# A spectral mixer and an MLP in one kernel: one row's sums moved to ScalarE, half a table loaded instead of computed, five fewer zero matmuls, and new instruction orders

## The chip, the cores and the metric

The kernel runs on one core of one Trainium2 chip. The metric is the device time of the whole program in microseconds (us). The kernel before took 348.37 us, the median of three runs (348.06 to 348.37). The profile is one execution of 348.26 us, of which it shows a span of 346.5 us. All times of the trace count from the start of that span.

## The reference: what is computed

The input x has 2048 positions of 512 features, in bf16. Two kinds of layer follow each other, twice:

```python
x = x + _A_ref(_layernorm(x, axis=-1), A_w_r, A_w_i)   # rfft2, times W, irfft2
x = x + _B_ref(_layernorm(x, axis=-1), B_w1, B_w2, B_w3, B_w4)
x = x + _A_ref(_layernorm(x, axis=-1), A_w_r, A_w_i)
x = x + _B_ref(_layernorm(x, axis=-1), B_w1, B_w2, B_w3, B_w4)
```

`_A_ref` takes a two-dimensional real Fourier transform of the normalised x, multiplies it by the complex weight W and transforms back. `_B_ref` normalises, multiplies by w1, applies GELU, shifts the four quarters of the features by -1, +1, -2 and +2 positions, multiplies by w2, adds x, normalises again and runs an MLP of width 1792 (w3, GELU, w4) with a second addition.

## The kernel before, in words

**Layout.** The 2048 positions lie as 128 partitions p by 16 rows q (position 16p+q). A "row" in this text is one q: a tile of 128 partitions by 512 features. The state x stays in SBUF for the whole run (`x_state`).

**The front.** The forward transform begins with a DFT over p: for each row TensorE multiplies the row by a 128x256 table T, which has first been scaled by the row's reciprocal standard deviation, so that the layernorm is folded into the table. `first_front` (L433) does this for the input. Its work is spelled as letters in the string ORDER_0, in program order, and every engine runs its own instructions in that order. `s5` takes the sums of row 5: either with BATCH_NORM_STATS on DVE (L273), or, for the rows in ON_ACT, with two ScalarE passes (a Copy at L349 and a Square at L285, each with an accumulated sum). `i5` aggregates the DVE form (L301). `f1` finishes the ScalarE form for the rows of group 1 with three small GpSimd instructions per row (L355 to L357). `S1` and `J1` are the square root on ScalarE (L361) and the reciprocal on DVE (L364) for group 1. GROUPS holds rows 0-3, 4-7, 8-11, 12-13 and 14-15. `Q5V` or `Q5A` writes the scaled table of row 5 on DVE (L379) or ScalarE (L381). `O2` is the front matmuls of the third row pair (L392, L394), followed for the first five pairs by FILL[k] matmuls on zeros (L257). `G2A` or `G2V` evicts that pair from PSUM into V on ScalarE or DVE (L150, L152). O7 and O8 are the single rows 14 and 15. The eviction of row 15 is split into G8A and G8V.

**Loads.** T comes over the ScalarE queue. The x rows and the W planes come over the SyncE queue. The other tables come over the GpSimd queue through `load_rest` (L180), which is called after the whole of ORDER_0: FA, two halves of TL, half of TR, and `double(0)`, which copies the first quarter of W into the other partitions. After them a one-element copy, the `gate` (L191), waits for the last scaled table. Behind the gate stand `turn_TL` for blocks 0-7, `double(1)`, `turn_TL` for blocks 8-15, `double(2)`, `double(3)` and the rest of TR. `turn_TL` (L230) makes the second plane of TL from the first: it swaps the two columns of every pair and negates one, in two GpSimd instructions (L233, L234).

**A layer.** `layer` (L490) runs twice. Its orders are ORDER_A and ORDER_B, in the same style, with the PSUM bank written after a dot. `d` is the DFT over features (L511), `t` its eviction, `q` the step over the row index against TL (L535: plane 0 and plane 1 of TL, one matmul each), `x` its eviction, `p` the product with W on DVE (L554), `b` the way back against TR (L565), `m` its eviction into hT, `D` and `Y` the inverse over features (L583) and its eviction, `P` the inverse over p (L595), `a` the addition to x with sums (L603), `s` the squares (L285), `r`, `e`, `i` and `n` the second layernorm, `T` a transposing DMA (L623), and `v`, `h`, `u`, `f`, `w`, `g`, `W`, `A` the matmuls, GELUs and additions of the two MLPs (L635 to L712). Units 0, 1, 14 and 15 hold one block of 64 frequencies, and units 2 to 12 hold two. Unit 10 covers blocks 10 and 11 and is thus the first user of the second half of TL in both orders. A suffix V or A names the engine of an eviction. `X4` is four matmuls on zeros (L257), and `N0` negates a part of TR on DVE (L770). `L` permutes a part of W for the second layer. The end of ORDER_A already makes the front of the second layer: `B` and `j` are stats, `S`, `J`, `Q` the scaled tables, `O` and `G` the front matmuls and their evictions. The first pairs use four plain matmuls (L404) and four DVE additions (`G0V` to `G4V`, L416) that need a copy of half the bank by ScalarE first (`G0A` to `G4A`).

At the very start, WAKE zero matmuls (L252, L257) keep TensorE occupied until the first scaled table is there.

Of the kernel before, what the change touches and what calls it, by code (L numbers as in the profile page):

```python
# [16 lines left out]
P = 128  # L17
# [4 lines left out]
NB = 16  # L22
# [6 lines left out]
def dft_tables():  # L29
# [14 lines left out]
    T = np.zeros((P, NH, 2, 2))  # L44
# [5 lines left out]
    T = T.reshape(P, P)  # L50
# [6 lines left out]
    FA = np.stack([cos, -sin], axis=1).reshape(2, P, 2, P, 2)[..., ::-1].transpose(1, 0, 4, 2, 3)  # L57
# [3 lines left out]
    G = G.transpose(2, 0, 1)  # L61
# [5 lines left out]
    for j in range(NH):  # L67
        for sg in range(2):
# [86 lines left out]
def load_all(K, A_x, A_w_r, A_w_i, B_w1, B_w2, B_w3, B_w4):  # L155
# [21 lines left out]
    K.TL = K.const.tile([P, 2, NB, P], BF16, name="TL")  # L177
    K.TR = K.const.tile([P, 3, NH, 64], BF16, name="TR")

    def load_rest(after):  # L180
        q = nc.gpsimd
        load_TL = lambda k: q.dma_start(K.TL[:, 0, 8 * k:8 * k + 8], dram["TL"][:, 8 * k:8 * k + 8])
        load_TR = lambda k: q.dma_start(K.TR[:, 0:2 + k, 16 * k:16 * k + 16], dram["TR"][:, 0:2 + k, 16 * k:16 * k + 16])
        double = lambda k: q.dma_start(K.W[1::2, :, 8 * k:8 * k + 8], K.W[0::2, :, 8 * k:8 * k + 8])
        table("FA", q)
        load_TL(0)
        load_TL(1)
        load_TR(0)
        double(0)
        gate = K.const.tile([1, 2], BF16, name="gate")  # L190
        q.tensor_copy(gate[:], after[0:1, 0, 0:2])  # L191
        turn_TL(K, slice(0, 8))
        double(1)
        turn_TL(K, slice(8, 16))
        double(2)
        double(3)
        load_TR(1)

    K.load_rest = load_rest
    K.load_G2 = lambda: nc.sync.dma_start(K.G[:], dram["G2"])  # L200

    def load_mlp():
# [230 lines left out]
def first_front(K):  # L433

    new_V(K)
    K.Tq = {}
    at = {q: (g, i) for g, rows in enumerate(GROUPS) for i, q in enumerate(rows)}
    L = [Stats(K, n=len(rows)) for rows in GROUPS]
    for g, rows in enumerate(GROUPS):
        if any(q in ON_ACT for q in rows):  # L440
            L[g].sums()
    ps = {}

    last_T = None
# [24 lines left out]
    def take(k, eng):
        take_V(K, FIRST[k], ps[k], eng, k == len(FIRST) - 1)  # L470

    def means(g):
        for i, q in enumerate(GROUPS[g]):
            if q in ON_ACT:
                L[g].from_means(i)

    table = {"s": stats, "i": aggr, "f": means, "S": lambda g: L[g].std(),
             "J": lambda g: L[g].invert(), "p": lambda g: L[g].rstd(), "Q": scale, "O": front, "G": take}
    for op in ORDER_0.split():
        if op[0] in "QG":  # L480
            table[op[0]](int(op[1:-1]), op[-1])
        else:
            table[op[0]](int(op[1:]))
    K.load_rest(last_T[:])
    K.load_mlp()
    spare = K.grp.tile([P, 4, 4, P], BF16, name="xT", bufs=4)
    K.nc.sync.dma_start_transpose(spare[:, 0, 0:1], K.zeros[:])
# [305 lines left out]
            table[op[0]](int(op[1:]))  # L793


WAKE = 35
FILL = {0: 3, 1: 3, 2: 2, 3: 2, 4: 2}
GROUPS = [[0, 1, 2, 3], [4, 5, 6, 7], [8, 9, 10, 11], [12, 13], [14, 15]]
ON_ACT = [1, 5]
FIRST = [[0, 1], [2, 3], [4, 5], [6, 7], [8, 9], [10, 11], [12, 13], [14], [15]]  # L800
UNITS = {b: [b, b + 1] if 2 <= b < 14 else [b] for b in (0, 1, 2, 4, 6, 8, 10, 12, 14, 15)}
ROOT = (0, 1)
# [5 lines left out]
PLAIN = 5  # L808
FLEX = "mGnotxY"
ORDER_0 = """  # L810
s0 s2 i0 s3 s1 i2 i3 f0 s4 S0 J0 i4 s5 Q1V Q0V Q3V Q2V s7 s6 i7 i6 s9 s11 O0 G0A f1 i9 S1 J1 s8 O1 G1A Q6A s10 Q7A i11
O3 i8 i10 Q5A s13 s12 Q4A O2 S2 J2 i13 Q10V G3A i12 Q9V s15 Q11A O5 S3 Q8A s14 i15 G2A O4 i14 S4 J3 Q12V G5A J4 Q15A
Q13V O6 Q14V G6A G4V O7 G7V O8 G8V G8A
"""
ORDER_A = """
X4.1 N0 d0.3 t0A d2.5 d1.7 t1A d4.0 t4A q0.2 x0A t2V q1.4 x1V p1 d10.6 d6.4 p0 t6V q2.1 t10A q4.6 x2A p2 x4A d12.3
b1.0 q6.1 p4 q10.6 t12A m1V b3.3 m3V x6A d8.4 d14.2 d15.0 x10A b5.6 t8A q8.4 p6 t14V t15A q12.0 b2.7 p10 m2V q14.2 m5A
x8A x12A q15.4 b0.6 m0A b10.7 m10A b4.1 m4A p8 b6.0 p12 m6V x14A p14 b11.7 x15A b9.1 p15 b13.6 m11A m9V m13A b7.3
b12.5 m12A b8.2 m8A b14.7 m14A m7V b15.5 m15A m15V D1.1 Y1V D0.5 D3.3 P2.7 a2 P3.2 a3 Y0A P0.1 a0 Y3A P7.4 P1.7 a1 s2
P6.2 s3 D2.0 s0 s1 a7 s7 a6 s6 D5.3 D4.6 r0 e0 Y2V P4.5 Y5A Y4A i0 n0V n1V P5.0 a4 s4 a5 s5 P11.2 D7.4 r1 P10.6 T0 Y7A  # L820
P8.3 e1 n3V n2V c1 T1 a11 a8 i1 D6.0 Y6A n5V P9.4 s11 P14.7 n4V n6V a9 n7V T2 P15.5 P12.3 a10 s8 a15 s9 a14 s10 P13.0
L0 v0.1 h0 a12 a13 v1.5 h1 T3 r2 c2 v3.4 n11V s12 c0 n10V T5 n8V n9V h3 s15 v2.3 h2 u0.5 L8 u3.0 u2.7 f0 L2 s14 f3
u1.5 f1 s13 r3 n12V n14V n15V f2 T4 v5.2 n13V h5 v4.1 u4.5 f4 E1 h4 u7.6 u6.1 f7 E3 u5.4 T7 k1 k0 f6 f5 k3 k2 E5 R0 c3
T6 v7.5 h7 u15.7 E0 v6.0 h6 E6 E4 u8.4 k7 o0V k5 o1V f15 E2 k6 o2V u10.3 o3V f10 k10 u12.7 u11.0 f8 u14.1 f14 U0 U1
u9.2 f9 k9 k8 w2.4 g2 f12 L9 E9 k4 R1 f11 k11 R2 w5.6 E11 g5 w4.2 g4 w1.0 u13.4 E8 o8V g1 o9V w3.5 g3 f13 E10 o10V
w0.1 g0 E7 o4A o7V w6.3 g6 W2.2 z0 o5V o6V A2 W3.7 A3 W1.6 A1 B1 W0.2 U3 U4 U2 E14 A0 w8.6 L13 B3 j3 g8 k14 o11V w12.1
g12 U5 w13.6 g13 w7.3 g7 w9.6 g9 k15 w10.3 g10 w18.0 w15.3 E12 g18 g15 w14.6 g14 w16.0 L11 w11.3 g11 g16 B2 W6.2 E13
W4.0 A6 w20.5 k13 L5 A4 B4 L12 W7.0 g20 w17.4 k12 R3 g17 o13A W5.1 A5 w19.5 g19 W9.2 o12V U6 j1 A7 B7 L15 j7 E15 j2 L7
o15V B6 W8.1 j6 B0 B5 j5 L3 W10.7 j0 S0 A10 B10 o14A U7 A9 j10 w25.4 g25 B9 Q2 j4 j9 A8 B8 L1 S1 Q1 Q4 w24.6 g24 W11.0
w21.2 g21 Q6 w22.6 j8 A11 L4 Q0 Q7 B11 j11 g22 L10 O0.3 w26.1 L14 g26 S2 Q11 G0A Q3 w23.6 w27.0 Q9 G0V g23 O1.2 G1A  # L830
Q10 G1V g27 W12.5 A12 O3.0 B12 W15.6 j12 Q5 G3A G3V A15 O2.2 G2A B15 Q8 j15 G2V S15 J15 Q15 W13.5 A13 B13 S12 W24.4
A24 j13 S13 J12 Q12 B24 J13 W14.5 Q13 A14 B14 O4.0 G4A O15.2 j14 S14 O5.6 G15V G15A O6.4 J14 Q14 O14.2 G4V G5A X3.7
G14V L6 G6A X4.1 G14A
"""
# [17 lines left out]


# [28 lines left out]
```

## Time and profile before

| | before |
|---|---|
| device time, median of 3 | 348.37 us |
| span of the profile | 346.5 us |
| TensorE (PE) busy | 337.5 us, 97% |
| ScalarE (ACT) busy | 192.0 us, 55% |
| VectorE (DVE) busy | 187.9 us, 54% |
| GpSimd (POOL) busy | 65.2 us, 19% |
| front: start to the first matmul of the first layer's `d` | 18.74 us |
| first layer, `d` to `b` (18.74 to 38.41) | 19.67 us |
| first layer, `D` and `P` up to the first `v` (38.41 to 53.12) | 14.71 us |
| its MLPs, and most of the second front (53.12 to 177.90) | 124.78 us |
| second layer, `d` to `b` (183.49 to 203.10) | 19.61 us |
| second layer, `D` and `P` up to the first `v` (203.10 to 218.40) | 15.30 us |

The share of TensorE is high in every stage, but a busy matmul engine is not always the one that sets the pace: the profile counts a matmul as busy for its whole latency (270 ns for 256 columns), while the next one starts much earlier. So a stage is read from the distances between starts, and from what the other engines had to do in it.

### The profile page before, as it was taken

The numbers are of one execution on the slowest core, as the hardware profiler recorded it, in microseconds if no ns is written. First come the engines' busy times: TensorE is split into PE (matmuls) and PEld (weight loads), VectorE is DVE, ScalarE is ACT, GpSimd is POOL, SyncE is SP. The second block draws the span as 40 slices with busy tenths as digits, with TensorE's granted clock in tenths as the row PEclk, the third lists the DMA queues.
The fourth block names the chain that finished last, engine by engine and source line by source line (L and its number), as shares of the span: only waits on it lengthen the run. The fifth ranks groups of instructions, "written<-read, shape, count | busy, mean of one in ns | idle before, by whom it ended". The sixth has DMA issues, their size and how long they took to land.

```text
span 346.5 us, 5563 instructions
## 1 busy us (share of the span) xinstructions
PE 337.5 (97%) x2116; PEld 190.0 (55%) x2134; DVE 187.9 (54%) x452; ACT 192.0 (55%) x342; POOL 65.2 (19%) x158
## 2 busy tenths in 40 slices
PE   8899999999999999999999999999999999999996
PEld 6778884444444444444577888444444444444453
DVE  5979798785435012877698959666614202002012
ACT  5979799666504633124357989954784531350320
POOL 2470047442200001032000003544305000000000
PEclk9999999999999999999999999999999999999999
DMA  7997965430221000210000002542103114100101
GB/s 265 290 328 246 359 132 111 80 63 7 49 45 30 0 2 0 55 38 1 0 2 0 2 2 53 95 88 50 23 2 61 30 45 104 19 30 17 45 23 53
DMA packets 45337, 24.64 MB, mean 71 GB/s; under 512 B 34944, under 2 KB 42240, under 8 KB 45312
## 3 DMA queue, kind: packets, MB, share of 16 engines
q1 hardware_dynamic: 43904, 20.00, 23.6%
q0 software_dynamic: 1168, 4.20, 3.4%
q8 instruction: 16, 0.26, 0.3%
q10 hardware_dynamic: 240, 0.10, 0.1%
q14 instruction: 9, 0.07, 0.1%
HBM read 11.67 MB, written 2.10 MB: 40 GB/s over the span
## 4 chain that ended last, share of the span: by engine, by line
PE 80%; DVE 8%; ACT 5%; DMA 4%; issue 2%; DVEq 0%; SPq 0%; ACTq 0%
PE ps L686 28%; PE ps L706 27%; PE ps L635 8%; PE ps L651 8%; PE ps L511 3%; DVE x_state L603 3%; DMA xT<-xn 2%; ACT V L152 2%; PE ps L583 2%; DVE PB L554 2%; PE ps L535 1%; DMA x_state<-in_A_x_dram 1%; DVE hT L150 1%; ACT X L152 1%; DMA T<-tab_T 1%
## 5 line engine op out<-in xcount | busy, mean ns | idle before, releaser
L693 ACT ACTIVATE gT<-ps 128x1024 bf16<-128x1024 f32 x56 | 56.3, 1022 | 93.9 <-PE ps L686 93.7
L686 PE MATMUL ps<-xT,w 128*128 128x512 bf16 x448 | 99.3, 379 | 0.1
L706 PE MATMUL ps<-w,gT 128*128 128x512 bf16 (+1 forms) x464 | 97.8, 366 | 0.6
L712 DVE TENSOR_TENSOR x_state<-ps,x_state 128x512 bf16<-128x512 f32 (+1 forms) x34 | 22.1, 657 | 108.6 <-PE ps L706 106.9
L706 PEld LDWEIGHTS <-gT 128*128 128x128 bf16 x476 | 46.5, 98 | 49.9
L686 PEld LDWEIGHTS <-w 128*128 128x128 bf16 x448 | 43.7, 98 | 52.9 <-DMA xT<-xn 0.6
L659 DVE SCALAR_TENSOR_TENSOR xn<-xn,ln_c,ps 128x512 bf16<-128x512 bf16 x32 | 23.2, 744 | 21.4 <-PE ps L651 13.1
L635 PE MATMUL ps<-xT,w 128*128 128x512 bf16 x128 | 28.8, 379 | 0.9 <-DMA xT<-xn 0.9
L651 PE MATMUL ps<-w,hT 128*128 128x512 bf16 x122 | 28.6, 379 | 0.3
L285 ACT ACTIVATE junk<-xn 128x512 bf16<-128x512 bf16 x32 | 19.7, 619 | 10.1 <-DVE xn L659 10.1
L642 ACT ACTIVATE hT<-ps 128x512 bf16<-128x512 f32 x32 | 18.1, 601 | 11.8 <-PE ps L635 11.8
L603 DVE SCALAR_TENSOR_TENSOR x_state<-ps,x_state 128x512 bf16<-128x512 f32 x32 | 20.5, 686 | 5.1 <-PE ps L595 5.1
L273 DVE BATCH_NORM_STATS2 ln_st<-x_state 128x6 f32<-128x512 bf16 (+1 forms) x31 | 20.2, 667 | 3.6 <-DMA x_state<-in_A_x_dram 3.2
L635 PEld LDWEIGHTS <-w 128*128 128x128 bf16 x128 | 12.4, 98 | 16.0 <-issue 1.6
L291 POOL TENSOR_SCALAR ln_mv<-ln_s 128x4 f32<-128x4 f32 x16 | 4.9, 304 | 85.3 <-DVE x_state L603 73.2
L651 PEld LDWEIGHTS <-hT 128*128 128x128 bf16 x128 | 12.5, 98 | 15.1
L554 DVE TENSOR_TENSOR PB<-X,W 128x2048 bf16<-128x2048 bf16 (+1 forms) x20 | 19.6, 1010 | 0.7 <-ACT X L152 0.5
L285 ACT ACTIVATE xn<-x_state 128x512 bf16<-128x512 bf16 x32 | 19.9, 624 | 0.2 <-DVE x_state L603 0.2
L293 POOL TENSOR_TENSOR ln_mv<-ln_s,ln_t 128x4 f32<-128x4 f32 x16 | 3.5, 217 | 75.4 <-ACT junk L285 70.0
L583 PE MATMUL ps<-G,hT 128*128 128x256 bf16 x128 | 15.4, 272 | 0.9 <-DVE hT L150 0.8
L565 PE MATMUL ps<-TR,PB 128*128 128x128 bf16 x256 | 16.1, 219 | 0.1
L565 PEld LDWEIGHTS <-PB 128*128 128x128 bf16 x256 | 14.8, 98 | 1.5 <-issue 1.2
(87 smaller groups left out, 390.0 us busy)
## 6 DMA issues: line engine op xcount, KB each, us to landing
w<-in_B_w_dram SPq DMA_DIRECT2D x2, 1792.0 KB, 12.1
W<-W POOLq DMA_DIRECT2D x4, 514.0 KB, 4.5
x_state<-in_A_x_dram SPq DMA_DIRECT2D x8, 256.0 KB, 4.8
out_dram<-x_state SPq DMA_DIRECT2D x15, 128.0 KB, 1.9
w<-in_B_w_dram SPq DMA_DIRECT2D x2, 512.0 KB, 6.2
W<-in_A_w_r_dram SPq DMA_DIRECT2D x7, 128.5 KB, 6.1
W<-in_A_w_i_dram SPq DMA_DIRECT2D x7, 128.5 KB, 6.5
TR<-tab_TR POOLq DMA_DIRECT2D x1, 768.0 KB, 6.8
```

The source lines that it names most:

```text
L285: K.nc.scalar.activation(out, src, ACT.Square, bias=0.0, scale=D ** -0.5, accum_out=self.s[:, i, 1:2])
L554: nc.vector.tensor_tensor(t, X.pop(u)[:, 0:2 * n].unsqueeze(1).to_broadcast([P, 2, 2 * n, 256]), K.W[:, :, 2 * u:2 * u + 2 * n, 1:257], op ...
L565: nc.tensor.matmul(oh, lhsT=pab[u][:, k, 2 * (b - u) + h, F * P:(F + 1) * P], rhs=K.TR[:, k:k + 2, 2 * b + h], start=(k == 0), stop=(k == 1))
L583: nc.tensor.matmul(o[:, i, e * 256:(e + 1) * 256], lhsT=M[:, F, e, 2 * m + i, :], rhs=K.G[:, F, e, :], start=(F == 0 and e == 0), stop=(F ...
L603: nc.vector.scalar_tensor_tensor(K.x[:, q, :], ps.pop(("P", q)), 1.0, K.x[:, q, :], op0=ALU.mult, op1=ALU.add, accum_out=ln[g].s[:, i, 0:1])
L635: nc.tensor.matmul(o[:, i], lhsT=K.w1[:, t, j * P:(j + 1) * P], rhs=xT[g][:, :, t, :], start=(t == 0), stop=(t == 3))
L651: nc.tensor.matmul(o, lhsT=K.hT[:, j, st:st + P], rhs=K.w2[:, j, :], start=(j == 0), stop=(j == 3))
L659: nc.vector.scalar_tensor_tensor(xn[:, q, :], xn[:, q, :], ln[q // 4].c[:, q % 4:q % 4 + 1], ps.pop(("u", n)), op0=ALU.mult, op1=ALU.add, ...
L686: nc.tensor.matmul(o[:, i], lhsT=K.w3[:, c, t * P:(t + 1) * P], rhs=xT3[g][:, :, c, :], start=(c == 0), stop=(c == 3))
L693: nc.scalar.activation(gT[g][:, 2 * j:2 * j + 2, :], ps.pop(("w", k)), ACT.Gelu_apprx_tanh, bias=0.0, scale=1.0)
L706: nc.tensor.matmul(o, lhsT=gT[g][:, t, i * P:(i + 1) * P], rhs=K.w4[:, t, d], start=(t == 0), stop=(t == 13))
L712: nc.vector.tensor_tensor(x, ps.pop(("W", n)), x, op=ALU.add)
```

## The change

1. **Row 9's sums.** ON_ACT gets row 9: its BATCH_NORM_STATS and aggregation leave DVE, and a Copy and a Square on ScalarE and three small GpSimd instructions (`f2`) come in.
2. **Half of the turned table.** The host makes a new table TL2, the second plane of TL for blocks 8-15. One DMA on the GpSimd queue loads it where the second `turn_TL` stood.
3. **Where the tables are loaded.** The first four table loads move into `load_tables`, which is called right after `f1`, so that `f2` stands behind them on the GpSimd queue and not ahead of them.
4. **WAKE** goes from 35 to 30 zero matmuls.
5. **New orders** for all three strings. In ORDER_0 the first table of row 1 moves from DVE to ScalarE, those of rows 4, 6, 7 and 15 from ScalarE to DVE, pair 4 is evicted by ScalarE, pair 6 by DVE and row 14 by ScalarE, as the last eviction. In ORDER_A the four zero matmuls at its start move to just ahead of the first `D`.

```diff
+    TL2 = TL.reshape(P, NB, 64, 2)[:, NB // 2:, :, ::-1] * np.array([-1.0, 1.0])
+    TL2 = TL2.reshape(P, NB // 2, P)
...
+    def load_tables():
         table("FA", q)
         load_TL(0)
         load_TL(1)
         load_TR(0)
+
+    def load_rest(after):
         double(0)
         gate = K.const.tile([1, 2], BF16, name="gate")
         q.tensor_copy(gate[:], after[0:1, 0, 0:2])
         turn_TL(K, slice(0, 8))
         double(1)
-        turn_TL(K, slice(8, 16))
+        q.dma_start(K.TL[:, 1, 8:16], dram["TL2"])
         double(2)
         double(3)
         load_TR(1)
...
+        if g == TABLES:
+            K.load_tables()
...
-WAKE = 35
+WAKE = 30
...
-ON_ACT = [1, 5]
+ON_ACT = [1, 5, 9]
+TABLES = 1
...
 ORDER_0 = """
-s0 s2 i0 s3 s1 i2 i3 f0 s4 S0 J0 i4 s5 Q1V Q0V Q3V Q2V s7 s6 i7 i6 s9 s11 O0 G0A f1 i9 S1 J1 s8 O1 G1A Q6A s10 Q7A i11
-O3 i8 i10 Q5A s13 s12 Q4A O2 S2 J2 i13 Q10V G3A i12 Q9V s15 Q11A O5 S3 Q8A s14 i15 G2A O4 i14 S4 J3 Q12V G5A J4 Q15A
-Q13V O6 Q14V G6A G4V O7 G7V O8 G8V G8A
+s0 s2 s3 i2 s1 f0 i0 i3 s4 S0 s5 f1 J0 Q3V Q0V Q2V Q1A O1 i4 s7 s9 s6 i7 i6 s11 s10 O0 S1 J1 Q7V Q4V G1A Q6V s8 G0A
+i11 f2 i10 Q5A i8 S2 s13 s12 O3 G3A J2 Q11A Q8A i12 i13 Q10V s15 S3 O2 G2A s14 i15 Q9V O5 O4 i14 J3 Q12V S4 G5A Q13V
+G4A O6 J4 Q14V O7 Q15V G6V O8 G8A G8V G7A
 """
 ORDER_A = """
-X4.1 N0 d0.3 t0A d2.5 d1.7 t1A d4.0 t4A q0.2 x0A t2V q1.4 x1V p1 d10.6 d6.4 p0 t6V q2.1 t10A q4.6 x2A p2 x4A d12.3
-b1.0 q6.1 p4 q10.6 t12A m1V b3.3 m3V x6A d8.4 d14.2 d15.0 x10A b5.6 t8A q8.4 p6 t14V t15A q12.0 b2.7 p10 m2V q14.2 m5A
...
-Q10 G1V g27 W12.5 A12 O3.0 B12 W15.6 j12 Q5 G3A G3V A15 O2.2 G2A B15 Q8 j15 G2V S15 J15 Q15 W13.5 A13 B13 S12 W24.4
-A24 j13 S13 J12 Q12 B24 J13 W14.5 Q13 A14 B14 O4.0 G4A O15.2 j14 S14 O5.6 G15V G15A O6.4 J14 Q14 O14.2 G4V G5A X3.7
-G14V L6 G6A X4.1 G14A
+d0.0 t0A d1.4 t1A d2.6 t2A q1.0 q0.2 x0A d4.4 t4A x1V p1 d10.1 N0 p0 q2.6 t10A q4.4 x4A d6.0 x2V p2 d12.3 p4 t6A q10.6
+q6.1 x6V t12A p6 b2.0 x10A p10 m2A d8.3 d14.6 t8A b3.1 m3A d15.7 t15A q8.3 x8A t14V q12.0 x12A p8 b1.5 b4.7 b7.6 m7A
...
+G3A G3V g26 G2A G2V W12.4 A12 B12 O0.2 j12 S12 L7 J12 Q12 W15.1 A15 B15 W13.5 G0A G0V j15 S15 W24.7 A13 B13 W14.5 J15
+j13 S13 A24 Q10 O4.6 G4A B24 J13 Q15 O15.1 Q13 Q11 A14 B14 j14 S14 G15V G15A O5.4 G5A J14 O6.0 Q14 O14.3 X3.5 G6A G4V
+X4.6 G14V G14A
 """
 ORDER_B = """
-d1.1 d4.3 t1V d15.7 t15V d8.0 t8V t4A q1.2 x1A p1 q4.6 x4A p4 d12.4 q15.2 t12A d10.6 x15A p15 t10A q8.0 q12.4 x12A
...
+d1.1 t1A d15.2 t15V d4.0 d8.6 t4A t8A q1.4 x1V q4.2 x4A p1 q15.0 d12.4 x15V p15 t12A d10.6 p4 q8.1 q12.3 b1.5 b5.0
...
 """
```

## The prediction

> **What bounds the kernel now.** I read the page's busy rows first, then busy time by stage, then the order-of-time view around the two places where TensorE (PE) does not set the pace. By stage (window and length, then busy time of PE, PEld, DVE, ACT, POOL, clock, DMA share, GB/s):
>
> ```profile
> 18.74:38.41 19.67, 19.15 (x258) 16.12 (x256) 17.78 (x23) 17.47 (x26) 5.30 (x7) 1.00 0.86 289
> 38.41:53.12 14.71, 14.47 (x128) 12.43 (x129) 12.39 (x35) 12.49 (x30) 3.81 (x13) 1.00 0.80 214
> 53.12:177.90 124.78, 124.31 (x601) 58.27 (x611) 71.91 (x183) 58.08 (x100) 25.08 (x55) 1.00 0.17 32
> 183.49:203.10 19.61, 19.17 (x256) 16.00 (x257) 18.02 (x22) 17.26 (x27) 0.00 (x0) 1.00 0.01 2
> 203.10:218.40 15.30, 14.51 (x128) 12.44 (x129) 11.14 (x33) 14.24 (x32) 4.51 (x15) 1.00 0.24 46
> 218.40:343.05 124.65, 124.16 (x581) 57.56 (x590) 36.46 (x93) 54.81 (x95) 19.11 (x48) 1.00 0.20 44
> ```
>
> Rows 3 and 6 are 249 us in which PE waits for nothing (0.5 us each is missing) and DVE and ACT are half idle: no order can shorten them, since the matmuls are the same. What is left is about 97 us. A 256-column matmul starts each 0.109 us (24 `D` in 2.62 us), so `D` and `P` cost 128 x 0.109 = 13.95 of the 14.71 us. `d`, `q` and `b` cost 64 x 0.109 + 64 x 0.066 + 128 x 0.056 = 18.3 of 19.67 us. All slack of the kernel is thus some 1.4 us in each `d`-`b` stage, about 1 us in each `D`-`P` stage, and the two fronts. The end of the first front, in order of time:
>
> ```profile
> 16.43 2.33 DVE L150 CAST V<-ps 128x1024 bf16<-128x1024 f32 x3
> 17.23 1.30 ACT L152 ACTIVATE V<-ps 128x1024 bf16<-128x1024 f32 x2
> 18.31 0.60 PE L257 MATMUL ps<-zeros 128*128 128x256 bf16 x4 [0.22 <-ACT V L152]
> 18.43 0.75 POOL L234 COPY TL<-TL 128x512 bf16<-128x512 bf16 x1
> 18.68 0.79 DVE L770 TENSOR_SCALAR TR<-TR 128x1024 bf16<-128x1024 bf16 x1
> 18.74 2.78 PE L511 MATMUL ps<-FA,V 128*128 128x256 bf16 x24
> ```
>
> `d` starts when the last eviction of V is done: DVE at 18.7, after working without a gap since 4.17. ACT had 0.9 us to spare. The end of the second front, on DVE:
>
> ```profile
> 177.93 0.43 DVE L712 TENSOR_TENSOR x_state<-ps,x_state 128x256 bf16<-128x256 f32 x1
> 178.53 0.29 DVE L379 TENSOR_SCALAR Tq<-T,ln_r 128x256 bf16<-128x256 bf16 x1
> 178.73 0.42 DVE L273 BATCH_NORM_STATS2 ln_st<-x_state 128x6 f32<-128x256 bf16 x1
> 179.25 0.29 DVE L379 TENSOR_SCALAR Tq<-T,ln_r 128x256 bf16<-128x256 bf16 x1
> 179.46 0.42 DVE L712 TENSOR_TENSOR x_state<-ps,x_state 128x256 bf16<-128x256 f32 x1
> ```
>
> From A24 at 177.93 to A14 at 179.46 DVE has no pause, and W14's matmuls end at about 179.26: both come due together. Behind A14 hang B14, j14, S14 and four ACT evictions, up to `d` at 183.49.
>
> [...] the wake matmuls start 0.212 us apart at first (17 in 3.60 us), and after the longest gap (1.18 us) matmuls still start 0.109 us apart. [...] this trace has 5.7 to 6.0 us for the TL halves under load, which I use.
>
> **The change part by part.**
>
> *Row 9, the Q's and the front's order.* On DVE a stats step takes 0.60 us (two in 1.20 from 14.07), an aggregation about 0.1, a scaled table 0.20 (0.87 for four). Before, DVE is through i14 at 15.49. In the new order Q9V is what pair 4 waits for. Up to it DVE does the same list less s9, i9, i14 (0.80) plus two tables (0.40): 15.1. Then O4, two fills, O6, O7, O8: 8 + 2 + 8 + 4 + 4 = 26 starts of 0.11 = 2.9, to 18.0. PSUM is read 0.2 us later. ACT is free (its sum: 1.3 more for row 9, three tables of 0.41 less, row 14's eviction 0.5 more, its former 0.9 us wait gone: 17.4 before the last two evictions) but has G8A (0.35) ahead of G7A (0.50): 18.2 + 0.85 = 19.05, `d` at 19.1. **+0.36.** f2 stands behind four table issues on GpSimd (8.72 to 11.35 as before), about 12.2 done; S2 is behind Q5A at 12.1 and waits at most 0.2, which is gone at J2 (13.4).
>
> *X4 and N0.* The fills at the start of ORDER_A went on while DVE finished; the same four now lie between the last `b` and the first `D`, where PE waited 0.45 us for m15 and the fills take 0.44. N0 moves to where GpSimd is done, but DVE then had 0.8 us idle. **0.**
>
> *WAKE.* PE reaches full rate after about 27 of them (10 of the second 18 at 0.213, then 0.109, add up to their 2.9 us). Thirty end near 7.1 and the first front matmul waits for its table until 7.9. [...] **0.**
>
> *TL2.* Its issue takes turn_TL's place: gate 16.5, turn to 19.1, double(1) 0.7, TL2 issued at 19.8, landed 5.8 later at 25.6. Its first user is q10, twelfth on PE in the new order: about 7.5 us behind `d`, 26.6 us. The 2.4 us of GpSimd it frees had nobody waiting. **0**, if it lands in time.
>
> *First d-b stage.* ACT evictions: six `t` doubles and four `x` doubles at 0.91, five singles at 0.50, twelve `m` at 0.497, m15 0.37: 17.9, against 16.9 before. It starts 0.7 after the first `d` and has now work at once (before it waited 0.71, 0.28 and 0.35 more): 18.6. I walk through the list and find pauses of about 0.9 (t2 waits for two-block d2, t4 and t10 for banks): 19.5, against 19.67. DVE has 1.3 less. **-0.1.**
>
> *D and P, both layers.* The sequence a, s, r, e, i, n to the first two transposes is in effect the same as before, and P ends at 52.97 with the transpose landing at 52.98. In layer two T3's 3.82 us stay on the path. **0.**
>
> *Second front.* From A24 to A14 the new DVE order has tables 10, 15, 13 and 11 and no J12 and 12: J15 comes before A24. Two tables more (0.40), a J of 0.17 less: A14 at 179.7. S14 and the evictions behind it follow unchanged. **+0.28.**
>
> *Second d-b stage.* t1 and t8 go to ACT, x1 and x15 to DVE. ACT's list is 17.55 against 17.15 but loses its 0.6 wait for q1; the walk ends 0.2 earlier. **-0.2.**
>
> *MLP stages.* PE-bound in both: **0.**
>
> Sum: 0.36 - 0.1 + 0.28 - 0.2 = +0.34; 348.37 + 0.34 = 348.7 us.
>
> **The rivals.** *Faster, 347.0.* The waits I walked into do not happen. If DVE alone ends the front it is 0.75 us shorter: it loses s9, i9 and row 14's eviction (0.60 + 0.1 + 0.65) and gains three tables (0.60). ACT without pauses would end the first d-b stage 1.0 us sooner (0.7 + 17.9 against 19.67), the second 1.4 (0.65 + 17.55 against 19.61), though PE's 18.3 plus the last eviction holds them to about 0.8 each. Together -2.35, 346.0 at best; some 60% of it gives 347.0. For it: the early ACT waits are in the profile and the new order fills them. Against: ACT is already full from 24.5 to 38.4 (13.73 of 13.90) and gets more work. *Slower, 350.0.* TL2 lands late. Under load the TR load took 7.4 and a W load 8.2 us; issued at 19.8 TL2 then lands at 27.2 to 28.0, and q10 and all of PE behind it waits 0.6 to 1.4 us. With a front and a second front at the upper end of my walks (+0.6, +0.4): 348.37 + 1.0 + 0.6, or +1.4: 350.0 to 350.8. For it: DMA is 0.97 to 1.19 busy from 19 to 22. Against: at 22 to 23 it falls to 0.23.
>
> **How the numbers follow.** My forecast, 348.7, gets 0.38, the faster case 0.33, the slower 0.29. The low end, 346.2, takes in all but the last of the faster case, and the high end, 350.3, half of the slower one. The band of 0.2% is 347.7 to 349.1 and holds the forecast: same 0.38, faster 0.33, slower 0.29.
>
> **What would show it.** Right: the first `d` of layer one near 19.1 with an ACT eviction of 128x512 just ahead of it; A14 about 0.3 later after A24; the d-b stages within 0.4 of 19.6; no PE wait for a DMA into TL; 124.7 us in each MLP stage. Wrong: `d` before 18.5, a d-b stage below 19.0, a PE wait on TL, or any PE wait in an MLP stage, where I assumed none.

## The result, and the profile after

The changed kernel takes 349.83 us, the median of six runs (349.03 to 350.30); the kernel before, run beside it, 348.30 us (six runs, 348.06 to 348.42). The ratio is 1.0044, with a 95% interval of 1.0031 to 1.0057: 0.44% slower. The forecast was 348.7 us and no measurable change. The time lies inside the stated range (346.2 to 350.3), but above the band that the forecast called the same (up to 349.1), and most of the lost time is in stages that the working priced at zero.

The windows view of the changed kernel, by the stages of the prediction (window and length, then busy time and number of instructions of PE, PEld, DVE, ACT and POOL, clock, DMA share, GB/s):

```profile
18.52:38.30 19.78, 19.62 (x260) 16.17 (x261) 16.50 (x20) 18.41 (x28) 3.83 (x7) 1.00 0.89 306
38.30:54.01 15.71, 14.39 (x129) 12.43 (x129) 12.16 (x38) 14.39 (x33) 5.48 (x17) 1.00 0.79 209
54.01:184.85 130.84, 130.53 (x662) 62.79 (x662) 75.48 (x198) 62.30 (x108) 23.07 (x51) 1.00 0.17 29
184.85:204.72 19.87, 19.32 (x256) 16.20 (x257) 16.82 (x20) 17.83 (x27) 0.00 (x0) 1.00 0.01 2
204.72:220.11 15.39, 14.49 (x128) 12.42 (x129) 12.53 (x36) 13.23 (x31) 2.45 (x10) 1.00 0.26 46
```

In the second row TensorE (PE) is busy 14.39 us, as before (14.47), but the stage takes 15.71 and not 14.71 us. PE has 1.3 us in which it does nothing. The stages of both profiles side by side (span 346.5 us before, 348.1 after):

| stage, us | before | after | difference | predicted |
|---|---|---|---|---|
| front, to the first `d` | 18.74 | 18.52 | -0.22 | +0.36 |
| first `d` to `b` | 19.67 | 19.78 | +0.11 | -0.1 |
| first `D` and `P`, to the first `v` | 14.71 | 15.71 | **+1.00** | 0 |
| first `v` to the first `w` | 26.76 | 27.22 | **+0.46** | 0 |
| first `w` to the second layer's `d` (with the second front) | 103.61 | 103.62 | +0.01 | +0.28 |
| second `d` to `b` | 19.61 | 19.87 | +0.26 | -0.2 |
| second `D` and `P` | 15.30 | 15.39 | +0.09 | 0 |
| second `v` to the end | 128.09 | 128.03 | -0.06 | 0 |
| sum | | | +1.65 | +0.34 |

What PE waits for (the waits view; us in total, times, longest), of the changed kernel:

```profile
PE ps L642 <- DMA xT<-xn: 1.2, 1, 1.2
PE ps L642 <- DVE x_state L610: 0.6, 1, 0.6
PE ps L518 <- DVE V L152: 0.6, 1, 0.6
PE ps L693 <- DMA xT<-xn: 0.2, 1, 0.2
```

and the answering line of the kernel before:

```profile
PE ps L635 <- DMA xT<-xn: 0.9, 2, 0.7
```

L642 (before L635) is `v`, L693 is `w`; both read xT, which a transposing DMA writes. Before, the two waits of `v` for it were 0.2 us (first layer) and 0.7 us (second layer), and `w` had none. Now the first `v` waits 1.2 us and the first `w` 0.2 us. There is no wait of PE for TL. The chain of waits says which transfer it is (start, length). After:

```profile
49.27 4.61 DMA xT<-xn
...
77.35 3.83 DMA xT<-xn
```

and before:

```profile
49.46 3.52 DMA xT<-xn
```

The second transposing DMA of the layer is issued 0.19 us earlier than before and lands 0.89 us later. So neither DVE nor ScalarE is late with its data: the transfer itself takes longer, from issue to landing. In all 14 kernels traced here, in both layers, the first `v` starts 0.135 us after the landing of the layer's second transposing DMA, with one exception (e13, first layer: 0.34), so this landing is what ends each `D`-`P` stage.

The waits view puts the second `v`'s 0.6 us down to DVE (the line with x_state), but that `v`, too, starts 0.135 us after a landing. In e6, below, the same DVE instruction ends at the same point of its stage (15.4 us in), while `v` starts there at 14.76.

The end of the first front in the timeline of the changed kernel (start, length; several instructions of a kind are merged):

```profile
15.57 2.90 ACT L154 ACTIVATE V<-ps 128x1024 bf16<-128x1024 f32 x4
...
16.93 1.56 DVE L152 CAST V<-ps 128x1024 bf16<-128x1024 f32 x2 [0.39 <-PE ps L399]
...
18.46 0.75 POOL L239 COPY TL<-TL 128x512 bf16<-128x512 bf16 x1
...
18.52 0.72 PE L518 MATMUL ps<-FA,V 128*128 128x256 bf16 x5 [0.59 <-DVE V L152]
```

ScalarE ends its four evictions at 18.47, DVE its two at 18.49, and `d` starts at 18.52 behind DVE. I had ScalarE end it at 19.05.

### The profile page after: what moved, and what is told of

It reads as the page before. It is cut to its first block, busy times and chain, and to the rows that moved or that the text cites. A ratio compares the mean times of both kernels' runs of the same rounds, so it can differ in the third digit from the quotient of the medians.

```text
span 348.1 us, 5592 instructions
## 1 busy us (share of the span) xinstructions
PE 337.3 (97%) x2129; PEld 188.8 (54%) x2129; DVE 183.4 (53%) x445; ACT 197.0 (57%) x351; POOL 62.3 (18%) x160
## 4 chain that ended last, share of the span: by engine, by line
PE 80%; DVE 11%; DMA 3%; ACT 2%; issue 2%; DVEq 0%; ACTq 0%
PE ps L693 28%; PE ps L713 27%; PE ps L642 8%; PE ps L658 6%; PE ps L518 2%; DVE x_state L610 2%; DMA xT<-xn 2%; PE ps L572 2%; PE ps L590 2%; DVE ln_st L278 2%; DVE PB L561 2%; PE ps L542 1%; DMA x_state<-in_A_x_dram 1%; ACT X L154 1%; PE ps L602 1%
## 5 line engine op out<-in xcount | busy, mean ns | idle before, releaser
L693 PE MATMUL ps<-xT,w 128*128 128x512 bf16 x448 | 99.6, 379 | 0.2 <-DMA xT<-xn 0.2
L713 PE MATMUL ps<-w,gT 128*128 128x512 bf16 (+1 forms) x476 | 99.7, 366 | 0.0
L693 PEld LDWEIGHTS <-w 128*128 128x128 bf16 x448 | 43.7, 98 | 53.1 <-DMA xT<-xn 0.7
L642 PE MATMUL ps<-xT,w 128*128 128x512 bf16 x128 | 28.6, 379 | 1.8 <-DMA xT<-xn 1.2
L642 PEld LDWEIGHTS <-w 128*128 128x128 bf16 x128 | 12.4, 98 | 17.0 <-issue 2.3
L278 DVE BATCH_NORM_STATS2 ln_st<-x_state 128x6 f32<-128x512 bf16 (+1 forms) x30 | 19.5, 665 | 3.6 <-DMA x_state<-in_A_x_dram 3.4
L154 ACT ACTIVATE TV<-ps 128x1024 bf16<-128x1024 f32 (+1 forms) x18 | 15.2, 890 | 2.7 <-PE ps L518 2.6
L518 PE MATMUL ps<-FA,V 128*128 128x256 bf16 x128 | 15.7, 273 | 0.8 <-DVE V L152 0.6
L602 PE MATMUL ps<-Y,Tinv 128*128 128x256 bf16 x128 | 15.4, 272 | 0.4 <-DVE x_state L610 0.3
```

The lines of the kernel that those rows point to most:

```text
L278: self.K.nc.vector.bn_stats(self.st[i][:, int(k)], src)
L518: nc.tensor.matmul(oi[:, 1 - h], rhs=K.FA[:, t, h], lhsT=V[:, 2 * t + h, 2 * b:2 * b + 2].rearrange("d b q c -> d (b q c)"), start=(t == 0 ...
L642: nc.tensor.matmul(o[:, i], lhsT=K.w1[:, t, j * P:(j + 1) * P], rhs=xT[g][:, :, t, :], start=(t == 0), stop=(t == 3))
L693: nc.tensor.matmul(o[:, i], lhsT=K.w3[:, c, t * P:(t + 1) * P], rhs=xT3[g][:, :, c, :], start=(c == 0), stop=(c == 3))
L713: nc.tensor.matmul(o, lhsT=gT[g][:, t, i * P:(i + 1) * P], rhs=K.w4[:, t, d], start=(t == 0), stop=(t == 13))
```

## The experiments

All are timed beside the kernel before, and a ratio is given with its 95% interval. The first seven put single parts of the change on the kernel before, or take single parts out of the changed one.

Their expectations name three theories, which I had formed on the trace of the changed kernel. **"Order"**: a new order is too tight for DVE or ScalarE and loses by itself, wherever it stands. **"Extra load"**: the load of TL2 pushes the later loads back (256 KB at the 366 GB/s that the kernel before moved from 19 to 22 us are 0.7 us). **"Instruction fetch"**: the DMA view of the changed kernel has a queue named "instruction" with 16 packets of 16 KB, of 0.88 to 1.39 us each. The theory takes them for reads of TensorE's instructions: the number of these sets when a read comes, and a transposing DMA that meets one lands about 1 us later (4.61 us for 3.52 ahead of the first `v`). Then parts that are free alone can lose together. A "read" below is a packet of a queue of that name.

**e1: the new front alone** (row 9 on ScalarE, `load_tables`, ORDER_0) on the kernel before.

```diff
-ON_ACT = [1, 5]
+ON_ACT = [1, 5, 9]
+TABLES = 1
-ORDER_0 = (before)
+ORDER_0 = (after)
```

> The kernel before with the new front alone: row 9's sums on ScalarE, the new ORDER_0, and the first table loads ahead of f2. The second turn_TL, 35 zero matmuls and the old orders of both layers stay. My theory (the front gained 0.2 us, the loss lies in the first layer's D-P stage and its order): 348.1, the first d at 18.5 instead of 18.74, 14.7 us from the first D to the first v. Rival (the front's shift moves the loads and the later transposes): first v at or after 53.4 and no gain, 348.3 or more.

Measured: 348.10 us, ratio 1.0001 [0.9991, 1.0011]; first `d` at 18.72 (before 18.74; expected 18.5). The front is worth nothing in either direction that can be told from zero; my +0.36 is not there.

**e2: the load of TL2 alone.**

```diff
-        turn_TL(K, slice(8, 16))
+        q.dma_start(K.TL[:, 1, 8:16], dram["TL2"])
```

> The kernel before with the second turn_TL replaced by the DMA of TL2, nothing else. My step (hidden): 348.3. Theory 'extra load' [...]: 348.8 to 349.3, with the first v at 53.8. Theory 'instruction fetch': no change of TensorE's count, 348.3; if a second read of instructions appears near 52.5, as in the kernel after, it is GpSimd's count that sets it, and the first v comes near 54.

Measured: 348.44 us, 1.0005 [0.9997, 1.0013]. Nothing that can be told from zero, so "extra load" (348.8 or more) falls. In the changed kernel the timeline of GpSimd shows the issue where the working had it:

```profile
19.80 0.57 POOL L199 DMA_DIRECT2D TL<-tab_TL  x1
```

It lands 5.4 us later, at 25.2, and no PE wait on it exists.

**e3: WAKE alone.**

```diff
-WAKE = 35
+WAKE = 30
```

> The kernel before with 30 instead of 35 zero matmuls at the start, nothing else. Theory 'order' and theory 'extra load': no difference, 348.3 within 0.15. Theory 'instruction fetch' (each transposing DMA that meets a 16 KB read of the instruction queue loses about 1 us, and TensorE's instruction count sets when the read comes): ten instructions fewer ahead, so the read near 49.7 comes some 0.5 us later and falls into the second transpose: its landing moves from 52.98 to about 53.5 or 53.9, and the time rises by 0.5 to 1.0 us.

Measured: 348.59 us, 1.0005 [0.9997, 1.0013]; first `d` at 18.74, the same as before. Alone it costs nothing that can be told from zero. "Instruction fetch" expected 0.5 to 1.0 us and missed: in the trace the 16 KB read did come later against the second transposing DMA (0.68 us behind its issue, for 0.27), but the landing only grew from 3.52 to 3.74 us.

**e4: ORDER_A alone.**

```diff
-ORDER_A = (before)
+ORDER_A = (after)
```

> The kernel before with the new ORDER_A alone. Theory 'order': the whole loss but the second layer's 0.3 is here, 349.5, with 15.7 us from first D to first v and a PE wait of about 0.4 ahead of the first w. Theory 'instruction fetch': the four fills that move stand ahead of the first D in both orders, the count ahead of the transposes is that of the kernel before and not of the kernel after, so the second transpose lands as before (14.7 us), and only the wait ahead of the first w is left, 348.7. Theory 'extra load': 348.3 to 348.7 as well.

Measured: 348.47 us, 1.0002 [0.9993, 1.0010]. Its first `d`-`b` stage is 20.03 us (+0.36), but the first `D`-`P` stage is 14.68 and `v` to `w` 26.82. The order by itself makes neither of the two large losses, and "order", which expected 349.5, falls in this form.

**e5: ORDER_B alone.**

```diff
-ORDER_B = (before)
+ORDER_B = (after)
```

> The kernel before with the new ORDER_B alone. My step was -0.2 us in the second d-b stage; the trace of the kernel after shows +0.26 there (19.87 against 19.61) and +0.09 in the stage that follows. Theory 'order': the d-b stage is 19.87 here too, and the time 348.6. Theory 'instruction fetch': the D-P stage is 14.8 to 15.4, by where the read falls, so 348.0 to 348.7.

Measured: 348.29 us, 1.0004 [0.9995, 1.0012]. The second `d`-`b` stage takes 19.87 us (+0.26) and the second `D`-`P` stage 14.78 (-0.52). Behind that, the second layer's `w` starts later and the end comes sooner (27.76 us from `v` to `w` and 100.48 on to the end, for 25.90 and 102.19). The parts nearly cancel. The -0.52 is a landing again: the layer's second transposing DMA takes 3.32 us, for 3.82 before. Before, an 8 KB read of the queue named "instruction" (see under e6) starts 2.5 us behind its issue; here it starts 3.9 us behind.

So no part costs anything measurable alone: the five differences of the medians add up to +0.5 us, not to +1.5.

**e7: the changed kernel with the old ORDER_A.**

```diff
-ORDER_A = (after)
+ORDER_A = (before)
```

> The kernel after with the old ORDER_A (new front, TL2, 30 zero matmuls and new ORDER_B stay). Theory 'order': the loss in the first layer is gone, 348.5. Theory 'instruction fetch': the old order with ten fewer TensorE instructions ahead is the case of the run with 30 zero matmuls alone, first D-P stage 14.9, no wait ahead of the first w; the second layer's own loss stays: 348.7. Theory 'extra load': 349.2 or more.

Measured: 348.12 us (347.86 to 348.30), 0.9993 [0.9984, 1.0001]. The whole loss is gone, with all the other parts in place. ORDER_A loses 1.7 us next to the other parts and nothing measurable alone. ("Instruction fetch" expected 348.7.)

**e6: the changed kernel with 35 zero matmuls.**

```diff
-WAKE = 30
+WAKE = 35
```

> The kernel after with 35 instead of 30 zero matmuls. Theory 'order' and theory 'extra load': as the kernel after, 349.8. Theory 'instruction fetch': the read comes some 0.5 us earlier in the stream of work, out of the second transpose, and the first D-P stage loses 0.5 to 1.0 us less: 348.9 to 349.3.

Measured: 348.88 us, 1.0017 [1.0010, 1.0024]. Five zero matmuls in the first eight microseconds regain 0.95 us of 1.53, and the profile shows where: `w` has no wait (26.83), and the second `D`-`P` stage is 14.76 for 15.39. The first `D`-`P` stage keeps its loss (15.65). "Instruction fetch" had the time about right (348.9 to 349.3) and the place wrong: it named the first `D`-`P` stage. The profiled execution took 349.77 us, more than the median, because its front was 0.8 us late from the landing of x on; the stages behind are read by their lengths.

A change at 1 us that acts at 80 and at 215 us, with no wait in between that could carry it, points to something that goes with the number of instructions. The DMA view of the trace has a candidate: the queue named "instruction", with packets of 16 KB (16 in the changed kernel; 0.88 to 1.9 us each over all traces). In the changed kernel 4258 instructions of TensorE are recorded, 266 for each of the 16. In each of the 14 traces, from the fifth read to the sixteenth, TensorE's recorded instructions advance by 252 to 256 per read on average (2785 in eleven reads in the changed kernel, 2790 before, with single steps of 230 to 286). A second queue of that name has packets of 8 KB, 9 or 10 in a trace.

The DMA view of the stretch 75.4 to 81.4 us, in which two transposing DMAs for the first `w` run (busy share of the DMA engines in tenths, 40 slices of 0.15 us, a packet's time counted where it starts; then queue, packets, MB, time that the packets took as a share of 16 engines). The changed kernel:

```profile
DMA  0000000579999900000069999999000399900000
...
q1 hardware_dynamic: 2112, 0.52, 85.3%
q8 instruction: 1, 0.02, 1.2%
q14 instruction: 1, 0.01, 0.3%
```

and e6, with five more zero matmuls:

```profile
DMA  0030000000000699999995200079999999500000
...
q1 hardware_dynamic: 2112, 0.52, 46.4%
q8 instruction: 1, 0.02, 1.0%
q14 instruction: 1, 0.01, 0.3%
```

The 2112 packets are the same, but they took nearly twice as long, and besides the reads no other transfer runs in the stretch. In the changed kernel the 16 KB read starts at 76.56, 1.15 us after the first of the two transposing DMAs was issued, and from 77.5 to 78.4, six slices, nearly no packet starts. In e6 the read is the lone digit near the left edge, at 75.85, ahead of the issue.

That leaves **"instruction fetch"**, that a read which falls into a transposing DMA stalls it and that the change moves reads into them, and **its rival**, that the new ORDER_A is too tight for DVE or ScalarE next to the other parts.

**e9: five more ScalarE instructions** (one column each) ahead of the first `D` of the kernel before, to see whether a count on ScalarE moves the 8 KB read that the changed kernel has at 52.5 us and the kernel before at 55.6. The two one-column activations of this kind in the trace of before take 0.194 us each.

```diff
-... m15A m15V D1.1 ...
+... m15A m15V z1 z1 z1 z1 z1 D1.1 ...
```

> The kernel before with five one-column ScalarE instructions more (0.2 us each), put where ScalarE waits 1.85 us for the first D. They change nothing that is computed. Theory 'order' and theory 'extra load': 348.3, since they lie in idle time. Theory 'instruction fetch', for ScalarE's own read: the one at 55.6 comes about 3 us earlier, as in the kernel after, meets the second transpose, and the first v comes at 53.6 to 54: 348.8 to 349.2.

Measured: 348.24 us, 0.9996 [0.9988, 1.0004]; that read stays at 55.6, and no stage moves by more than 0.2 us. "Instruction fetch" expected 348.8 or more, with the read about 3 us earlier, and missed: it is not ScalarE's count that places this read.

**e10: old ORDER_A and 35 zero matmuls in the changed kernel.**

```diff
-WAKE = 30
-ORDER_A = (after)
+WAKE = 35
+ORDER_A = (before)
```

> The changed kernel with the old ORDER_A and with 35 zero matmuls, as before. If the loss is in the new ORDER_A alone (in what it meets), this is the changed kernel with old ORDER_A again: 348.1 us, first v within 3.9 us of the issue of the second transposing DMA, first w without a wait, second D-P near 14.8 us. If 30 zero matmuls cost something by themselves, it is faster than that kernel's 348.12 by 0.3 or more: 347.8.

Measured: 348.24 us, 0.9996 [0.9988, 1.0004]; second `D`-`P` stage 14.75, no wait ahead of `w`. As e7: with the old ORDER_A, 30 or 35 makes no measurable difference.

**e11: the changed kernel with the front of before.**

```diff
-ON_ACT = [1, 5, 9]
-ORDER_0 = (after)
+ON_ACT = [1, 5]
+ORDER_0 = (before)
```

> The changed kernel with the front of before (ORDER_0, row 9 and the place of the table loads as before); TL2, WAKE 30 and the new ORDER_A and ORDER_B stay. If the front is what ORDER_A must meet to lose, the first v comes within 3.9 us of the issue of the second transposing DMA and the time is 348.4 to 348.7. If it isn't, the 8 KB instruction read stays at 52 to 53 us, the first v comes 4.7 us after that issue, and the time is 349.5 or more.

Measured: 349.23 us (348.66 to 350.36), 1.0024 [1.0013, 1.0035]. Between the two cases: the 8 KB read is back at 55.6 and the first `D`-`P` stage is 14.66, but `w` waits 0.58 us and the second `D`-`P` stage takes 14.96. In this profile, taken from one of the faster executions (348.84), the first `v` has no loss without the new front; the first `w` has.

**e12: the changed kernel with GpSimd turning the second half of TL.**

```diff
-        q.dma_start(K.TL[:, 1, 8:16], dram["TL2"])
+        turn_TL(K, slice(8, 16))
```

> The changed kernel with the second half of the turned table made by GpSimd again; the new front, WAKE 30 and the new orders stay. If the load of TL2 is what ORDER_A must meet to lose, the first v comes within 3.9 us of the issue of the second transposing DMA and the time is 348.4 to 348.7; if it isn't, 4.7 us and 349.5 or more.

Measured: 349.92 us (348.63 to 350.57), 1.0038 [1.0026, 1.0050]. TL2 has no measurable part in the loss. The profiled execution is the fastest of the twelve (348.63): its first `D`-`P` stage is 14.88, so its profile does not show all that the median loses.

**e13: the changed kernel with 25 zero matmuls.**

```diff
-WAKE = 30
+WAKE = 25
```

> The changed kernel with 25 zero matmuls. If the stalls come from where TensorE's instruction reads fall, five instruction pairs fewer move every read by about 0.5 us and with it the waits: the wait ahead of the first w and the second D-P stage (15.39 us in the changed kernel, 14.76 with 35) differ from the changed kernel's by 0.3 us or more in one of them, and the time is off its 349.83 by 0.4 us or more in either direction. If the new orders are simply too tight for DVE or ScalarE, nothing moves: 349.8, give or take 0.3, with a front up to 0.3 us longer.

Measured: 349.81 us, 1.0034 [1.0021, 1.0047]. The time did not move, as the rival had it, but everything under it did, and the front by twice its allowance. The 16 KB read leaves the second transposing DMA (from 49.95 to 52.55 us, when its data have come), which now lands in 3.0 us for 4.6, and the first `D`-`P` stage falls from 15.71 to 14.36 us. The next read falls deeper into the transposes for `w`, and `v` to `w` rises from 27.22 to 27.81. The front goes up by 0.62 to 19.14. Together -1.35 + 0.59 + 0.62 = -0.14. The equal times are three moves that cancel. The front's part is in PE's timeline of e13:

```profile
1.01 4.43 PE L262 MATMUL ps<-zeros 128*128 128x256 bf16 x25 [1.01 <-DVE zeros L253]
8.18 0.37 PE L397 MATMUL ps<-Tq,x_state 128*128 128x256 bf16 x1 [2.75 <-DVE Tq L384]
8.35 0.42 PE L399 MATMUL ps<-Tq,x_state 128*128 128x256 bf16 x1
...
11.07 0.27 PE L399 MATMUL ps<-Tq,x_state 128*128 128x256 bf16 x1
```

The first front matmuls start 0.21 us apart, and only near 11 us 0.11 apart. With 30 zero matmuls they start 0.11 apart from 7.88 on. The windows view of e13 (window and length, PE busy and number, granted clock, DMA share, GB/s) shows the clock behind it:

```profile
4.20:5.40 1.20, 1.20 (x11) 1.00 0.92 319
7.60:10.90 3.30, 2.72 (x13) 0.50 0.93 308
11.10:13.00 1.90, 1.90 (x20) 1.00 0.87 256
```

The full pace was there in the last zero matmuls (11 in the 1.20 us of the first row): 25 of them at 0.21 us apart would take some 5.3 us, and they took 4.43. Behind the pause of 2.75 us it is gone, and the granted clock is 0.50. With 30 zero matmuls the pause is 1.38 us, and the granted clock is 1.00 from 7.80 to 10.90. What a pause between these two lengths does isn't shown.

**What the kernels say together.** The two transposing DMAs for the first `w` (the first issued at 73.5 to 76.2 us, the second some 2 us later), the 16 KB read next to the first of them, and the wait ahead of `w`:

| kernel | zero matmuls | ORDER_A | read after the issue, us | landings, us | PE wait, us |
|---|---|---|---|---|---|
| before | 35 | old | -0.60 | 3.4, 3.1 | 0 |
| e3 | 30 | old | -0.56 | 3.4, 3.1 | 0 |
| e7 | 30 | old | -0.33 | 3.9, 3.1 | 0 |
| e10 | 35 | old | -0.51 | 3.4, 3.0 | 0 |
| e4 | 35 | new | -0.43 | 3.4, 3.0 | 0 |
| e6 | 35 | new | -0.33 | 3.4, 3.1 | 0 |
| after | 30 | new | +1.15 | 5.0, 3.8 | 0.2 |
| e11 | 30 | new | +1.25 | 5.3, 4.2 | 0.6 |
| e12 | 30 | new | +1.28 | 4.9, 3.8 | 0.2 |
| e13 | 25 | new | +1.70 | 5.1, 4.0 | 0.4 |

The read comes in every kernel. With it ahead of the issue, the first landing takes 3.4 us (3.9 in e7); with it 1.1 to 1.7 us behind, 4.9 to 5.3. It gets there where the new ORDER_A and fewer than 35 zero matmuls meet, and in no kernel that has only one of them.

The second layer splits in the same way among the kernels with the new ORDER_B, but there it is the first transposing DMA's issue that is longer where the read comes with it: 1.41 to 1.93 us for 1.23 or 1.24. SyncE issues the second one 0.1 us after that (at 216.75 in the changed kernel, behind an issue from 214.71 to 216.64), and `v` follows its landing:

| kernel | read after the first issue, us | first issue lasts, us | second landing, us into the stage | `D`-`P` stage, us |
|---|---|---|---|---|
| e5 | -1.78 | 1.24 | 14.65 | 14.78 |
| e6 | -1.87 | 1.23 | 14.63 | 14.76 |
| e7 | -1.62 | 1.23 | 14.63 | 14.77 |
| e10 | -1.87 | 1.24 | 14.61 | 14.75 |
| e11 | 0.00 | 1.41 | 14.83 | 14.96 |
| e12 | 0.00 | 1.70 | 14.98 | 15.11 |
| e13 | +0.10 | 1.92 | 15.28 | 15.41 |
| after | +0.50 | 1.93 | 15.26 | 15.39 |

DVE and ScalarE are not what differs: up to `v`, each of their instructions in this stage starts at the same point of the stage in the changed kernel and in e6, to within 0.02 us.

All 14 traces together have 448 transposing DMAs of the two layers. 219 of them have no instruction read, of 16 or of 8 KB, from 1 us ahead of their issue to 4 us behind it, and all of these land in 3.02 to 3.27 us. Eight have a 16 KB read 1.1 to 2.35 us behind, and all of these land in 4.6 to 5.3 us. With the read 2.4 to 2.9 us behind, 6 of 28 take 4.7 to 4.9 us and the others at most 3.2. (In e6's view the packets of an undisturbed one start from 1.2 to 2.5 us behind the issue.) None of the 448 takes over 3.45 us without a read in that stretch. The kernel before has a late landing too, of 4.63 us at 47.6 us, but there nothing on the path waits for it.

**What stays open.** The changed kernel's first `v` loses more than these two places. In its profile and in e6's, the second transposing DMA meets a 16 KB read (0.7 us behind its issue) and, as its data end, an 8 KB read at 52.5 and 53.3 us. It lands in 4.6 us. The 16 KB read alone is not enough: before, e1 to e5, e7 and e9 to e11 have it 0.3 to 1.0 us behind the issue too, with their 8 KB read after 55 us, and land in 3.5 to 3.8. Nor is the 8 KB read: e12 has it at 52.7 us, an issue of 1.23 us (2.4 to 2.5 in the two) and a landing of 3.8, and e13 has it at 52.5 us and lands in 3.0. Only the two that have both, and a long issue, take 4.6, which is too few to call the pair the cause. Which engine's count that 8 KB read goes with, and what moves it by 3 us in the kernels that have both the new front and the new ORDER_A, was not found.

Nor was it shown why nearly no transposing packet starts for 0.9 us behind a read, or why five zero matmuls move a read against the work by up to 2.4 us where they last about 0.5 (starts 0.109 us apart). A part of that is the pace of the work: near 76 us a matmul starts each 0.216 us (24 in 5.18), so five are worth 1.1 us there. Each kernel has one trace, of one execution, while the times of a kernel spread by up to 2.4 us (e6: 347.7 to 350.2), so how often a read meets a transfer in other executions isn't known. The link from read to stall rests on these counts and on the moves by WAKE; a kernel without reads was not tried.

No version beats the kernel before by more than the interval: e7 comes nearest, at 0.9993 [0.9984, 1.0001].

## Why the prediction was right and where it was wrong

- **Front, +0.36: wrong in size and sign.** The step that failed is "26 starts of 0.11 = 2.9, to 18.0" and G8A and G7A behind them, 19.05. DVE was through Q9V at 15.07, as reckoned. But four of the 26 starts, those of row 8, didn't wait for Q9V (they started from 14.63 on, row 9's at 15.21); the last front matmul started at 17.65. And the first eviction did not wait for the last matmul: ScalarE began its last two at 17.59, not at 18.2. They took 0.88 us for 0.85. The change is -0.22 in this profile and -0.02 in e1; the fronts of before, e1 to e5, e7 and e9 to e12 lie between 18.46 and 18.82 whatever their order.
- **WAKE, 0: right alone (e3), wrong in the whole.** The working asked only what PE does until 7.9 us. The number of instructions ahead of everything else was no quantity in it. It put the pause at 0.8 us, from 7.1 to 7.9; the thirty ended at 6.50, since their starts are 0.109 us apart from the 21st on and not, as before, from the 28th. That a pause leaves the clock alone was my estimate, and the trace of before shows it for 1.18 us only. It held for 30 zero matmuls (1.38 us) but not for 25 (2.75 us, e13).
- **TL2, 0: right**, with its issue at 19.80 and its landing, predicted 25.6 and measured 25.2 (e2, e12).
- **First `d`-`b`, -0.1: the sign was wrong by little.** The term that was off is ScalarE's work: 18.41 us for my 17.9. It stood idle for 1.4 us, start and pauses together, for my 0.7 and 0.9. The stage became 19.78 for 19.5; other kernels with the new ORDER_A have 19.78 to 20.08. (By the working's own terms, 19.5 for 19.67 is -0.2 rather than -0.1, and the 18.3 of the matmuls is 18.4. The trace of before has its 0.066 and 0.056: 16 `q` in 1.04 us from 30.16, 96 starts of `b` in 5.35 us from 32.39.)
- **First `D` and `P`, 0: the step that failed most**, by 1.00 us. "P ends at 52.97 with the transpose landing at 52.98" took the landing of before, 3.52 us, as fixed. The two meet to within 0.01 us, so every lengthening of that transfer is on the path; it grew to 4.61. That the landing can depend on what else is read at that moment was no term of the sum. In the second layer "T3's 3.82 us stay on the path" failed in the same way: the landing is 3.3 us with the new ORDER_B (e5).
- **MLP stages, 0: wrong by +0.46 at one place.** "PE-bound in both" left out the first `w`, which waits for two transposes. PE's wait there is the prediction's own sign of being wrong ("any PE wait in an MLP stage"). The rest of the MLPs is as predicted (103.61 and 103.62).
- **Second front, +0.28: not there.** A24 to A14 took 1.51 us for 1.53 before. The next lines, of DVE's timeline in the changed kernel, show A24, a table, three tables, and A14. The matmuls behind W14 start at 180.62 (179.26 before), A14 starts 0.20 us after that in both kernels, and `d` 4.03 us after A14 in both. "Both come due together" was the failed step: PE's W14 releases A14, and DVE had room for its two tables. (The working's own terms, 0.40 less 0.17, give +0.23 rather than +0.28.)

```profile
179.31 0.40 DVE L719 TENSOR_TENSOR x_state<-ps,x_state 128x256 bf16<-128x256 f32 x1
179.63 0.28 DVE L384 TENSOR_SCALAR Tq<-T,ln_r 128x256 bf16<-128x256 bf16 x1
...
180.22 0.66 DVE L384 TENSOR_SCALAR Tq<-T,ln_r 128x256 bf16<-128x256 bf16 x3
180.82 0.42 DVE L719 TENSOR_TENSOR x_state<-ps,x_state 128x256 bf16<-128x256 f32 x1
```

- **Second `d`-`b`, -0.2: wrong sign**, +0.26 in every kernel with the new ORDER_B (19.87 or 19.88). I let the walk end earlier because one wait of 0.6 us of ScalarE fell away. Its work rose to 17.83 us for the 17.55 reckoned (17.26 before), and its idle time fell only from 2.35 to 2.04. **Second `D` and `P`, 0**: the order gains 0.52 (e5), and the read, by the longer issue, takes it back (15.39).

Of the rivals, the slower one came nearest in time, 350.0, for none of its reasons: TL2 was not late and no front grew. Its cause, a transfer that lands late under other traffic, was the right kind at the wrong transfer. That the time fell inside the range is partly luck, since errors of both signs cancelled: actual less predicted is +1.46 at the two waits for transposes, +0.67 in the `d`-`b` stages and -0.85 in the two fronts. Without the last, it would have been 350.7 us.

## What to carry to other kernels

Where an engine's work ends within tenths of a microsecond of a transfer's landing, the forecast must ask what else uses the DMA engines at that moment. Here the list had to include the queue named "instruction": with its 16 KB packets 1.1 to 1.7 us behind the issue, the first transfer for `w` took 4.9 to 5.3 us for 3.4. Look for that queue in the DMA view and compare its packets' times with the issues of the transfers on the path. A part that is free alone can cost in the whole (ORDER_A: nothing measurable alone, 1.7 us next to the other parts), so remove parts from the finished kernel as well as adding them to the old one.

## What the runs showed of the hardware that was not expected

- The 16 KB packets of the queue named "instruction" come in line with TensorE's count (one per 252 to 256 recorded instructions on average, from the fifth on, in each of the 14 traces) and take 0.88 to 1.9 us each. A transposing DMA with such a packet 1.1 to 2.35 us behind its issue lands in 4.6 to 5.3 us, for 3.02 to 3.27 without any packet of 16 or 8 KB from 1 us ahead to 4 us behind; in the changed kernel nearly none of the transposing packets starts from 77.5 to 78.4 us.
- The issue of a transposing DMA takes 1.23 to 1.42 us when no 16 KB read is near, and up to 2.5 us when one starts within the first 0.7 us of it (1.70 before, 2.52 in the changed kernel). In the second layer's `D`-`P` stage the next transposing DMA is issued 0.1 us behind the end of that.
- Five zero matmuls at the start moved reads against the work: by 1.5 us near 76 us and 2.4 us near 215 us (e6 to the changed kernel), by 2.0 us near 50 us (the changed kernel to e13). The first two go with 0.95 us of the time.
- TensorE's granted clock was 0.50 behind a pause of 2.75 us (e13), and 1.00 behind one of 1.38 us (the changed kernel).
- Kernels with the new ORDER_A next to the other parts vary more from execution to execution (349.0 to 350.3 us, e11 348.7 to 350.4, e12 348.6 to 350.6, and e6, with 35 zero matmuls, 347.7 to 350.2) than the changed kernel with the old ORDER_A (347.9 to 348.3).
